# Newton's iteration for both head groups of a batch in one chain, with landmark and U transposes as whole tiles

## The chip, the cores and the metric

The kernel runs on one core of a Trainium2 chip. The metric is the device time of one execution in microseconds (us); lower is better. Before the change it is 927.63 us, the median of three runs (926.26 to 928.45).

## What is computed

Three stages follow each other; all arrays are float32.

```
Nystrom attention, batch 4, heads 8, seq 576, head_dim 64, m = 32:
  q_lm, k_lm = mean of q, k over 18 neighbouring rows        (32 landmarks a head)
  A = softmax(q k_lm^T)   B = softmax(q_lm k_lm^T)   C = softmax(q_lm k^T)
  Z = B^T / (norm1(B) * norminf(B) + 1e-6);  6 times: Z = 2 Z - Z B Z
  x = A Z C v                       -> 2304 tokens x 512
two gated layers, d_model 512, d_ff 1536:
  x = (silu(x wg1) * (x wv1)) wo1;  out = (sigmoid(x wg2) * (x wv2)) wo2
```

The factor U = Z C v (32 x 64 a head) is multiplied into the first layer's weights, so that the first layer reads A straight: x wg1 = A (U wg1).

## The kernel before

A batch has two head groups g of four heads, and 32 rows of each head fill a quarter of the 128 partitions. The work on one (b, g) is the generator `attention`, cut in two parts. The front part, called F in the order of work, does this: sums of 18 rows on VectorE (`lm`, L107); the landmark sums transposed on TensorE by two ordinary matmuls with the identity (`lt`, L111), so that the result stands on both partition halves; nine 128x128 transposes of k and nine of q (`tp`, L121); scores of C (`cs`), of B (`bm`) and of A (`as`); the exponentials; transposes of C's exponentials (`et`, L207); and C v (`cv`, L213). The back part, B, normalises B and finds the two norms with small VectorE instructions (L220 to L237), runs Newton's iteration (`nw`, L240 to L261), transposes U (`ut`, L265) into `UT[b]`, and finishes A (`a_steps`, L144 to L158) between the iterations.

Newton's iteration is carried on [Z^T-like 32 columns | U 64 columns] together, 96 columns a head. One product is four matmuls of 32x32 weights, one for each head, each on its own 32 rows and 32 columns of the array; one VectorE instruction of 96 columns reads the result and makes the next operand. There are seven products and seven such instructions to a chain, and each needs the one before.

After B of both groups, `uw_steps` (L391, word U, tile `pu`) multiplies UT[b] by the chunk of the first layer's weights: eight matmuls of 64x32 weights and 512 columns. The weights of two heads lie on the two partition halves, and `half` (L386) says which half a head has; for heads 4 to 7 `load_in` (L307) loads the halves swapped. Then G (`gv1_steps`, tiles `pg`, `pv`) and O (`o1_steps`, tile `po`) are the first layer, in matmuls of 128x128 weights and 288 columns, three for each product (high and low parts). The second layer has the same form.

The order in which the work is recorded is written out by hand as words (L570): letter, then (b, g) for F and B, or (chunk, batch) for U, G and O; words joined by + take turns.

```
first = (
    "I0+F00 F01 B00+F10 B01 U00 F11 J0 B10 G00 I1 F20 U10 J1 O00 G10 B11 O10 U01 G01 F21 U11 "
    "B20+F30+B21 O01 G11 B30+F31 U02 O11 G02 B31 U12 O02 G12 U03 O12 G03 U13 O03 G13"
)
```

A scheduler then orders the recorded instructions on each engine by its own costs; that order is fixed when the program runs. I and J wait for the conversion of weights, which fills in (`wfill`) between steps. Attention tiles in PSUM use the tags gv (3 banks), n (1), o (2) and a (2). All loads are issued on SP.

Of the kernel before, what the change touches and what calls it, by code (L numbers as in the profile page):

```python
# [5 lines left out]
F32 = mybir.dt.float32  # L6
# [8 lines left out]
def nystrom_moe_kernel(tc, q, k, v, wg1, wv1, wo1, wg2, wv2, wo2, out):  # L15
    nc = tc.nc
# [39 lines left out]
    UT = [cst.tile([P, H, M], F32, tag=f"ut{b}", name=f"ut{b}") for b in range(B)]  # L56
# [33 lines left out]
    def attention(b, g):  # L90
# [3 lines left out]
        def small(tag, shape, bufs=2):  # L94
            return att.tile(shape, F32, tag=tag, name=f"{tag}{nm_}", bufs=bufs)

        def pst(shape, nm):

            tag = "n" if nm in ("nw", "ut") else "a"
            if b == 0:  # L100
                tag = {"tp": "gv", "cs": "o", "as": "o", "nw": "no"[g], "ut": "no"[g]}.get(nm, tag)
            return ptile(shape, tag, f"{nm}_{nm_}")

        def lm_steps(which):
            src = inq[which, b, g]
            lm = small("lm", [P, D])
            nc.vector.tensor_reduce(lm, src.rearrange("p u d -> p d u"), axis=AX.X, op=ALU.add)  # L107
            yield
            ps = pst([P, P], "lt")
            for w in range(2):  # L110
                mm(ps[D * w:D * w + D], lm, ident)  # L111
            bdt = small("bd" + which, [P, 2, P], 1)
# [14 lines left out]
        def a_scores(bdk, qT, s):  # L127

            amx = small("amx", [P, L])
            for i0, i1 in ((0, 5), (5, NU)):  # L130
                ps = pst([P, 5, 2 * M], "as")
                for i in range(i0, i1):
                    for h in range(4):
                        hs = slice(M * h, M * h + M)
                        mm(ps[hs, i - i0].rearrange("p (w m) -> p w m", w=2), qT[:, i, hs], bdk[:, :, hs])
                x = flat(ps[:, 0:i1 - i0]).rearrange("p (u m) -> p u m", m=M)
                us = slice(2 * i0, 2 * i1)
                nc.vector.tensor_reduce(amx[:, us], x, axis=AX.X, op=ALU.max)
                nc.vector.tensor_tensor(s[:, us], x, amx[:, us, None].to_broadcast([P, 2 * (i1 - i0), M]),
                                        op=ALU.subtract)  # L140
                nc.scalar.activation(s[:, us], s[:, us], AF.Exp)
                yield

        def a_steps(s):  # L144
            asm = small("asm", [P, L])
            nc.vector.tensor_reduce(asm, s, axis=AX.X, op=ALU.add)
            nc.vector.tensor_scalar(asm, asm, 1e-9, None, op0=ALU.add)
            nc.vector.reciprocal(asm, asm)
            yield
            nc.vector.tensor_tensor(s, s, asm[:, :, None].to_broadcast([P, L, M]), op=ALU.mult)  # L150
            yield
            at = small("at", [P, S], 1)
            nc.vector.transpose(out=at, in_=flat(s))
            hi, lo = AH[:, 8 * g + b], AH[:, 8 * g + 4 + b]
            nc.scalar.copy(hi, at)
            nc.vector.tensor_tensor(lo, at, hi.bitcast(F32), op=ALU.subtract)
            AT[b, g, 0] = hi
            AT[b, g, 1] = lo  # L158
            yield
# [4 lines left out]
        cmx = small("cmx", [P, 2])
        csm = small("csm", [P, 2])
        nmx = small("nmx", [P, 1])
        e = small("e", [P, 3, 2, M, 3], 1)
# [16 lines left out]
        bs = small("bs", [P, M])  # L184
        bmx = small("bmx", [P, 1])
        bsm = small("bsm", [P, 1])
        ps = pst([P, M], "bm")
# [22 lines left out]
        ps = pst([P, D], "cv")  # L210
# [4 lines left out]
        nc.vector.tensor_scalar(BC[:, M:M + D], ps, rc, None, op0=ALU.mult)  # L215
        load_next(b, g, "v")
        yield
        yield "back"
# [3 lines left out]
        nc.vector.tensor_scalar(BC[:, 0:M], bs, bsm, None, op0=ALU.mult)  # L222
        bmt = small("bmt", [P, M])
        nc.vector.transpose(out=bmt, in_=BC[:, 0:M])
        nrm = small("nrm", [P, 2])
        nc.vector.tensor_reduce(nrm[:, 0:1], BC[:, 0:M], axis=AX.X, op=ALU.add)
        nc.vector.tensor_reduce(nrm[:, 1:2], bmt, axis=AX.X, op=ALU.add)
        yield
        nb = small("nb", [P, 2, M])
        nc.vector.tensor_copy(nb, nrm[:, :, None].to_broadcast([P, 2, M]))  # L230
        nbt = small("nbt", [P, 2, M])
        nc.vector.transpose(out=flat(nbt), in_=flat(nb))
        nmax = small("nmax", [P, 2])
        nc.vector.tensor_reduce(nmax, nbt, axis=AX.X, op=ALU.max)
        rr = small("rr", [P, 1])
        nc.vector.tensor_scalar(rr, nmax[:, 0:1], nmax[:, 1:2], 1e-6, op0=ALU.mult, op1=ALU.add)
        nc.vector.reciprocal(rr, rr)  # L237


        def prod(x):  # L240
            ps = pst([P, 96], "nw")
            for h in range(4):
                hs = slice(M * h, M * h + M)
                mm(ps[hs], x[hs, 0:M], x[hs])
            return ps

        ga = a_steps(sx)
        ps = prod(BC)
        RW = small("rw", [P, 96], 4)
        nc.vector.tensor_scalar(RW, ps, rr, None, op0=ALU.mult)  # L250
# [12 lines left out]
        ps = pst([P, P], "ut")
# [4 lines left out]
        yield from ga  # L268
# [385 lines left out]
```

## Time and profile before

| what | value |
|---|---|
| median of the runs | 927.63 us |
| the profiled execution's own time | 925.59 us |
| span of its instructions on the core | 923.8 us |
| TensorE busy | 896.7 us (97%) |
| VectorE busy | 549.0 us (59%) |
| ScalarE busy | 389.3 us (42%) |
| mean granted TensorE clock | 0.987 of full |

PE is TensorE's matmuls, PEld its weight loads, DVE is VectorE, ACT ScalarE, POOL GpSimd, SP SyncE, which issues the loads. Busy time of PE is a modelled one, since matmuls overlap: where rows follow each other without a gap, the time from one start to the next is what a group takes. A float32 matmul gives two records in the trace, a float32 transpose and a matmul of the float32r type one. The granted clock is a share of 2.4 GHz; at 0.50 the array runs at 1.2 GHz.

### The profile page before, as it was taken

The page shows a single profiled execution, that of the slowest core. Times are in us where ns is not written, and L with a number is a line of the kernel's source. Part 1 is how long each engine was busy: PE and PEld are TensorE (multiplying, and loading weights), DVE is VectorE, ACT ScalarE, POOL GpSimd, SP SyncE. Part 2 cuts the span into 40 slices and gives each one's busy share as a digit, 9 for nine tenths or more (in the row PEclk, how much of TensorE's full clock was granted, in tenths as well). Part 3 has the DMA queues.
Part 4 walks back from the last instruction along what each step waited for, and adds up shares of the span by engine and source line. Part 5 has one row for each costly group of instructions (what it writes and reads, how often), then busy time and mean ns, then how long its engine had stood idle before and what let it go on. Part 6 is the DMA issues. An engine that isn't in the chain of part 4 may idle for free.

```text
span 923.8 us, 16229 instructions
## 1 busy us (share of the span) xinstructions
PE 896.7 (97%) x6664; PEld 747.5 (81%) x6664; DVE 549.0 (59%) x1165; ACT 389.3 (42%) x833; POOL 0.7 (0%) x6
## 2 busy tenths in 40 slices
PE   6789999999999999999999999999999999999997
PEld 4456866677989989899898888888888888888886
DVE  7799958647677668858972135347237336323243
ACT  6569655545645336536753343125116114111111
POOL 0000000000000000000000000000000000000000
PEclk9689999999999999999999999999999999999999
DMA  8664211003322104302101013004004000000132
GB/s 275 194 195 159 83 53 47 8 1 92 120 64 89 48 2 128 102 1 92 47 3 44 1 46 92 0 1 137 1 1 137 1 0 23 1 1 1 46 92 69
DMA packets 26698, 57.67 MB, mean 62 GB/s; under 512 B 3840, under 2 KB 6912, under 8 KB 26624
## 3 DMA queue, kind: packets, MB, share of 16 engines
q1 hardware_dynamic: 24896, 54.28, 18.9%
q10 hardware_dynamic: 1728, 2.36, 1.1%
q8 instruction: 52, 0.85, 0.4%
q14 instruction: 22, 0.18, 0.1%
HBM read 51.90 MB, written 4.72 MB: 61 GB/s over the span
## 4 chain that ended last, share of the span: by engine, by line
PE 91%; DVE 5%; ACT 2%; DMA 1%; issue 1%; SPq 0%; DVEq 0%; ACTq 0%
PE po L62 33%; PE pg L62 24%; PE pv L62 24%; PE pu L62 3%; PE nw L62 2%; PE tp L121 2%; DVE lm L107 1%; PE cs L62 1%; DMA kin<-in_k_dram 1%; PE cv L62 1%; PE as L62 1%; PE et L207 1%; PE lt L62 0%; DVE hl L327 0%; DVE cv L295 0%
## 5 line engine op out<-in xcount | busy, mean ns | idle before, releaser
L62 PE MATMUL po<-hh,wo 128*128 128x288 f32 x768 | 162.8, 303 | 1.0 <-DVE uw L327 0.7
L492 DVE TENSOR_TENSOR hf<-hf,pv 128x512 f32<-128x512 f32 (+1 forms) x60 | 38.0, 634 | 194.1 <-PE pv L62 191.5
L62 PE MATMUL po<-wo,h 128*128 128x512 f32 x648 | 152.2, 390 | 0.0
L62 PEld LDWEIGHTS po<-wo,h 128*128 128x128 f32 x648 | 121.2, 188 | 25.3 <-ACT h L326 0.3
L62 PEld LDWEIGHTS po<-hh,wo 128*128 128x128 f32 x768 | 123.2, 188 | 20.5 <-issue 13.7
L62 PE MATMUL pg<-AH,w 128*128 128x512 f32 (+1 forms) x480 | 136.2, 368 | 0.0
L62 PE MATMUL pv<-AH,w 128*128 128x512 f32 (+1 forms) x480 | 136.1, 368 | 0.0
L62 PE MATMUL po<-hl,wo 128*128 128x288 f32 x384 | 115.1, 300 | 0.3 <-DVE hl L327 0.3
L491 ACT ACTIVATE hf<-pg 128x512 f32<-128x512 f32 (+1 forms) x60 | 33.1, 552 | 165.2 <-PE pg L62 157.0
L62 PE MATMUL pg<-AH,uw 128*128 128x288 f32 x576 | 98.9, 298 | 2.5 <-ACT uw L326 2.4
L62 PEld LDWEIGHTS pg<-AH,w 128*128 128x128 f32 x480 | 87.4, 189 | 15.4
L62 PEld LDWEIGHTS pv<-AH,w 128*128 128x128 f32 x480 | 87.1, 189 | 14.9
L62 PE MATMUL pv<-AH,uw 128*128 128x288 f32 x576 | 95.9, 296 | 0.0
L62 PEld LDWEIGHTS pg<-AH,uw 128*128 128x128 f32 x576 | 83.2, 188 | 9.2 <-ACT uw L326 5.3
L326 ACT CAST h<-hf 128x512 fp32r<-128x512 f32 (+1 forms) x60 | 34.6, 576 | 123.6 <-DVE hf L492 123.6
L513 DVE TENSOR_TENSOR oacc<-po,oacc 128x512 f32<-128x512 f32 x90 | 61.9, 691 | 41.1 <-PE po L62 39.9
L62 PEld LDWEIGHTS pv<-AH,uw 128*128 128x128 f32 x576 | 82.7, 188 | 2.9 <-ACT bdk L114 0.8
L62 PE MATMUL pg<-x1l,w 128*128 128x512 f32 x192 | 74.8, 389 | 0.0
L62 PE MATMUL pv<-x1l,w 128*128 128x512 f32 x192 | 74.8, 389 | 0.0
L62 PEld LDWEIGHTS po<-hl,wo 128*128 128x128 f32 x384 | 72.3, 188 | 2.7 <-issue 1.1
L447 DVE TENSOR_TENSOR acc<-po,acc 128x288 f32<-128x288 f32 x128 | 55.8, 453 | 16.8 <-PE po L62 16.0
L419 ACT ACTIVATE sg<-pg 128x288 f32<-128x288 f32 x96 | 39.1, 407 | 51.8 <-PE pg L62 51.2
(106 smaller groups left out, 1093.9 us busy)
## 6 DMA issues: line engine op xcount, KB each, us to landing
raw<-in_moe_w_out_dram SPq DMA_DIRECT2D x24, 512.0 KB, 4.3
raw<-in_moe_w_gate_dram SPq DMA_DIRECT2D x36, 256.0 KB, 3.2
raw<-in_moe_w_val_dram SPq DMA_DIRECT2D x36, 256.0 KB, 3.5
kin<-in_k_dram SPq DMA_DIRECT2D x8, 576.0 KB, 4.7
qin<-in_q_dram SPq DMA_DIRECT2D x8, 576.0 KB, 5.5
vin<-in_v_dram SPq DMA_DIRECT2D x8, 576.0 KB, 4.6
raw<-in_moe_w_gate_dram SPq DMA_DIRECT2D x24, 128.0 KB, 2.9
raw<-in_moe_w_val_dram SPq DMA_DIRECT2D x24, 128.0 KB, 3.0
```

Source lines behind the costliest of these rows:

```text
L62: nc.tensor.matmul(o, l, r, start=start, stop=stop, skip_group_check=True)
L107: nc.vector.tensor_reduce(lm, src.rearrange("p u d -> p d u"), axis=AX.X, op=ALU.add)
L121: nc.tensor.transpose(ps[:, j], flat(src[:, 2 * u:2 * u + 2]), ident)
L207: nc.tensor.transpose(ps[:, j, :], flat(e[:, r // 2, r % 2]), ident)
L326: nc.scalar.copy(hi, x)
L419: nc.scalar.activation(sg, pss[0], AF.Silu)
L447: nc.vector.tensor_tensor(sl, ps, sl, op=ALU.add)
L491: nc.scalar.activation(h, pss[0], AF.Sigmoid)
L492: nc.vector.tensor_tensor(h, h, pss[1], op=ALU.mult)
L513: nc.vector.tensor_tensor(acc, ps, acc, op=ALU.add)
```

## The change

One back part now serves both head groups of a batch. Its tiles have the group as another dimension: B's rows `bs` (128x2x32), `BC` (128x2x96), the iterate `RW` (128x2x96), `rr` (128x2). One product is eight matmuls: four for group 0 and four for group 1, on the same four places of the array. One VectorE instruction of 192 columns follows. The words B00, B01 and so on become B0 to B3, and stand after both fronts. In the front part A's scores move behind C v. The sum of landmarks is written twice side by side by a ScalarE copy, so that one 128x128 transpose gives both halves. U of both groups is one 128x128 tile and one transpose; so group 0 lies on partitions 0 to 63 and group 1 on 64 to 127, and the first layer's weights are loaded that way, by four transfers of 64 rows each for every tile pair. UT[b] has half the columns that it had.

```
-            lm = small("lm", [P, D])
-            nc.vector.tensor_reduce(lm, src.rearrange("p u d -> p d u"), axis=AX.X, op=ALU.add)
+            lm = sm("lm", [P, 2, D])
+            nc.vector.tensor_reduce(lm[:, 0], src.rearrange("p u d -> p d u"), axis=AX.X, op=ALU.add)
+            nc.scalar.copy(lm[:, 1], lm[:, 0])
-            for w in range(2):
-                mm(ps[D * w:D * w + D], lm, ident)
+            nc.tensor.transpose(ps, flat(lm), ident)
...
         def prod(x):
-            ps = pst([P, 96], "nw")
-            for h in range(4):
-                hs = slice(M * h, M * h + M)
-                mm(ps[hs], x[hs, 0:M], x[hs])
+            ps = pst(b, [P, 2, 96], "nw")
+            for g in range(2):
+                for h in range(4):
+                    hs = slice(M * h, M * h + M)
+                    mm(ps[hs, g], x[hs, g, 0:M], x[hs, g])
             return ps
-        RW = small("rw", [P, 96], 4)
-        nc.vector.tensor_scalar(RW, ps, rr, None, op0=ALU.mult)
+        RW = sm("rw", [P, 2, 96], 3)
+        nc.vector.tensor_tensor(RW, ps, rr[:, :, None].to_broadcast([P, 2, 96]), op=ALU.mult)
...
-        for w in range(2):
-            mm(ps[D * w:D * w + D], UU, ident)
-        nc.vector.tensor_copy(flat(UT[b][:, 4 * g:4 * g + 4]), ps)
+        nc.tensor.transpose(ps, flat(UU), ident)
+        nc.vector.tensor_copy(flat(UT[b]), ps)
...
-            if layer == 0 and kk >= 2:
-                nc.sync.dma_start(t[0:D, j], x[D:P])
-                nc.sync.dma_start(t[D:P, j], x[0:D])
+            if layer == 0:
+                for g in range(2):
+                    r0 = D * (4 * g + kk)
+                    nc.sync.dma_start(t[D * g:D * g + D, j], w[r0:r0 + D, 2 * FC * c:2 * FC * (c + 1)])
...
-        for h in range(H):
-            rows = slice(D * half(h), D * half(h) + D)
-            mm(pss[h // 4][M * (h % 4):M * (h % 4) + M, :], UT[b][rows, h, :],
-               W1[c][rows, h // 2].rearrange("p a b -> p (a b)"))
+        for g in range(2):
+            rows = slice(D * g, D * g + D)
+            for h in range(4):
+                mm(pss[g][M * h:M * h + M, :], UT[b][rows, h, :], W1[c][rows, h].rearrange("p a b -> p (a b)"))
...
-        "I0+F00 F01 B00+F10 B01 U00 F11 J0 B10 G00 I1 F20 U10 J1 O00 G10 B11 O10 U01 G01 F21 U11 "
-        "B20+F30+B21 O01 G11 B30+F31 U02 O11 G02 B31 U12 O02 G12 U03 O12 G03 U13 O03 G13"
+        "I0+F00 F01 B0+F10 U00 F11 J0 B1 G00 I1 F20 U10 J1 O00 G10 O10 U01 G01 F21 U11 "
+        "B2+F30 O01 G11 F31 U02 O11 G02 B3 U12 O02 G12 U03 O12 G03 U13 O03 G13"
```

How the order of instructions moves is shown at two places. The numbers in the rows' names: the first after the tile's name is the head group (for `pu`, `pg`, `po` the batch, then the group or token half); an x at the end counts instructions of one row.

TensorE before, at the end of batch 0's second chain, up to U of chunk 0 and batch 0 (`pu`):

```order
L62 MATMUL cv_0_714<-vin_0_490,eT_0_703 32x64 x24
L62 MATMUL nw_1_796<-rw_1_790 32x96 x4
L62 MATMUL lt_1_843<-ident,lm_1_841 64x128 x2
L121 MATMUL tp_1_850<-ident,kin_1_345 128x128 x2
L62 MATMUL nw_1_803<-rw_1_801 32x96 x4
L121 MATMUL tp_1_850<-ident,kin_1_345 128x128
L121 MATMUL tp_1_855<-ident,kin_1_345 128x128 x3
L62 MATMUL nw_1_810<-rw_1_808 32x96 x4
L121 MATMUL tp_1_860<-ident,kin_1_345 128x128 x3
L62 MATMUL lt_1_869<-ident,lm_1_867 64x128 x2
L62 MATMUL ut_1_817<-ident,uu_1_815 64x128 x2
L62 MATMUL pu_0_0_821<-w_0_97,ut_82 32x512 x4
```

TensorE after the change, at the same place:

```order
L62 MATMUL nw_0_634<-rw_625 32x96 x8
L62 MATMUL bm_0_687<-bdk_0_519,bdq_0_613 32x32 x4
L185 MATMUL et_0_699<-ident,e_0_670 96x128 x2
L287 MATMUL ut_0_650<-ident,rw_643 128x128
L185 MATMUL et_0_699<-ident,e_0_670 96x128
L185 MATMUL et_0_704<-ident,e_0_670 96x128 x3
L62 MATMUL cv_0_709<-vin_0_447,eT_0_698 32x64 x12
L62 MATMUL pu_0_0_783<-w_0_97,ut_82 32x512
L62 MATMUL cv_0_709<-vin_0_447,eT_0_698 32x64 x12
L62 MATMUL as_0_739<-bdk_0_519,kq_0_628 32x64 x20
L62 MATMUL as_0_763<-bdk_0_519,kq_0_628 32x64 x16
L62 MATMUL pu_0_0_783<-w_0_97,ut_82 32x512 x3
```

Before, the landmarks and key transposes of F11 (`lt_1`, `tp_1`) stood ahead of `pu`, and F10 was done; now none of F11 stands ahead of it, and half of C v and all of A's scores of F10 stand behind its first matmul.

TensorE before, in batch 2, where the chains of both groups (`nw_0`, `nw_1`) and the front of batch 3's group 0 take turns:

```order
L62 MATMUL nw_1_2107<-rw_1_2088 32x96 x4
L121 MATMUL tp_0_2235<-ident,qin_0_1287 128x128 x3
L62 MATMUL po_0_1_2395<-hh_0_1_1821,wo_0_98 128x288
L62 MATMUL po_0_1_2395<-hl_0_1_1822,wo_0_98 128x288
L62 MATMUL po_0_1_2395<-hh_0_1_1843,wo_0_98 128x288 x2
L62 MATMUL cs_0_2244<-kq_0_2101,bdq_0_2192 32x288
L62 MATMUL nw_0_2118<-rw_0_2095 32x96 x4
L62 MATMUL cs_0_2244<-kq_0_2101,bdq_0_2192 32x288 x3
L62 MATMUL cs_0_2250<-kq_0_2101,bdq_0_2192 32x288
L62 MATMUL nw_1_2131<-rw_1_2112 32x96 x4
L62 MATMUL cs_0_2250<-kq_0_2101,bdq_0_2192 32x288 x3
```

TensorE after the change, in the same batch (here `nw_0` is both groups):

```order
L62 MATMUL nw_0_2054<-rw_2045 32x96 x8
L135 MATMUL tp_0_2111<-ident,qin_0_1288 128x128
L62 MATMUL cs_0_2127<-kq_0_1993,bdq_0_2071 32x288 x4
L62 MATMUL po_0_1_2283<-hh_0_1_1745,wo_0_98 128x288 x2
L62 MATMUL po_0_1_2283<-hl_0_1_1746,wo_0_98 128x288
L62 MATMUL po_0_1_2283<-hh_0_1_1767,wo_0_98 128x288 x2
L62 MATMUL nw_0_2074<-rw_2063 32x96 x8
L62 MATMUL po_0_1_2283<-hl_0_1_1768,wo_0_98 128x288
L62 MATMUL po_0_1_2291<-hh_0_1_1745,wo_0_98 128x288
L62 MATMUL cs_0_2133<-kq_0_1993,bdq_0_2071 32x288 x4
L62 MATMUL po_0_1_2291<-hh_0_1_1745,wo_0_98 128x288
L62 MATMUL nw_0_2092<-rw_2083 32x96 x8
```

Groups of four `nw` matmuls became groups of eight, half as many; the scores `cs` that were cut into one and three matmuls stand whole.

## Rows read from the trace of the kernel before

**Rows 1.** The page: TensorE's busy time, and the chain that ended last by engine.

```profile
PE 896.7 (97%) x6664; PEld 747.5 (81%) x6664; DVE 549.0 (59%) x1165; ACT 389.3 (42%) x833; POOL 0.7 (0%) x6
PE 91%; DVE 5%; ACT 2%; DMA 1%; issue 1%; SPq 0%; DVEq 0%; ACTq 0%
```

**Rows 2.** Windows: stretch and its length, busy us of each engine, granted clock, DMA.

```profile
core 0: us, PE busy (x) PEld busy (x) DVE busy (x) ACT busy (x) POOL busy (x), PEclk, DMA share, GB/s
0.00:60.10 60.10, 42.50 (x665) 27.60 (x665) 47.03 (x114) 34.00 (x84) 0.70 (x6) 0.80 0.71 223
36.00:44.00 8.00, 8.00 (x70) 4.19 (x60) 3.81 (x16) 3.16 (x8) 0.00 (x0) 0.50 0.51 147
60.10:85.60 25.50, 24.59 (x322) 14.28 (x320) 23.89 (x62) 23.17 (x47) 0.00 (x0) 1.00 0.49 157
85.60:226.50 140.90, 138.85 (x1649) 106.09 (x1649) 101.18 (x272) 80.91 (x188) 0.00 (x0) 1.00 0.20 58
```

**Rows 3.** Timeline of TensorE: start, duration, line, tiles, count; batch 0's first U.

```profile
60.14 1.52 PE L62 MATMUL pu<-w,ut 64*32 64x512 f32 x16
```

**Rows 4.** Timeline of TensorE: one Newton product between matmuls of O.

```profile
105.57 0.29 PE L62 MATMUL po<-hh,wo 128*128 128x288 f32 x1
105.85 0.37 PE L62 MATMUL nw<-rw 32*32 32x96 f32 x8
106.15 0.40 PE L62 MATMUL po<-hh,wo 128*128 128x288 f32 x1
106.39 0.29 PE L62 MATMUL po<-hl,wo 128*128 128x288 f32 x1
106.52 0.42 PE L62 MATMUL po<-hh,wo 128*128 128x288 f32 x2
```

**Rows 5.** Timeline of TensorE: scores of C, one half of them, and both.

```profile
127.73 0.69 PE L62 MATMUL cs<-kq,bdq 128*32 128x288 f32 x8
...
87.49 1.18 PE L62 MATMUL cs<-kq,bdq 128*32 128x288 f32 x16
```

**Rows 6.** Timeline of TensorE: a landmark transposition; one, three and six transposes.

```profile
107.01 0.44 PE L62 MATMUL lt<-ident,lm 128*64 128x128 f32 x4
107.38 0.44 PE L121 MATMUL tp<-ident,kin 128*128 128x128 f32 x2
...
116.06 0.27 PE L121 MATMUL tp<-ident,kin 128*128 128x128 f32 x1
...
160.81 0.55 PE L121 MATMUL tp<-ident,kin 128*128 128x128 f32 x3
...
166.71 0.87 PE L121 MATMUL tp<-ident,kin 128*128 128x128 f32 x6
```

**Rows 7.** Timeline of TensorE: a cut piece of C's scores; A's scores and C v whole.

```profile
145.54 0.67 PE L62 MATMUL cs<-kq,bdq 128*32 128x288 f32 x2
...
178.98 1.26 PE L62 MATMUL as<-bdk,kq 128*32 128x64 f32 x72
...
98.83 0.88 PE L62 MATMUL cv<-vin,eT 96*32 96x64 f32 x48
```

**Rows 8.** Groups of VectorE: Newton's step, and a reduction for the norms; count, busy, mean ns.

```profile
L255 DVE SCALAR_TENSOR_TENSOR rw<-rw,nw 128x96 f32<-128x96 f32 x40 | 10.0, 251 | 9.4 <-PE nw L62 8.9
L226 DVE TENSOR_REDUCE nrm<-bc 128x1 f32<-128x32 f32 x8 | 1.2, 147 | 0.0
```

**Rows 9.** Timeline of TensorE: two Newton products of one chain that follow each other.

```profile
57.88 0.37 PE L62 MATMUL nw<-rw 32*32 32x96 f32 x8
...
58.78 0.37 PE L62 MATMUL nw<-rw 32*32 32x96 f32 x8
```

**Rows 10.** Timeline of TensorE: U, one matmul of it alone, and all eight.

```profile
126.28 1.04 PE L62 MATMUL pu<-w,ut 64*32 64x512 f32 x2
...
116.90 1.09 PE L62 MATMUL pu<-w,ut 64*32 64x512 f32 x16
```

**Rows 11.** Waits of SP's own queue: line, waited for, us in total, times, longest.

```profile
SPq L322 <- ACT cv L293: 379.9, 14, 63.4
```

More of the change, by code (lines that the diff above doesn't have):

```diff
@@ L54, in nystrom_moe_kernel @@
         nc.vector.memset(pmask[64 * h:64 * h + 64, h:h + 1], QSC)
-    UT = [cst.tile([P, H, M], F32, tag=f"ut{b}", name=f"ut{b}") for b in range(B)]
+    UT = [cst.tile([P, 4, M], F32, tag=f"ut{b}", name=f"ut{b}") for b in range(B)]
     AT = {}
@@ L125, in lm_steps @@
             return bdt, t
[L127 to L132, printed above, removed]
-                    for h in range(4):
-                        hs = slice(M * h, M * h + M)
[L135 to L159, printed above, removed]
         bdk, kT = yield from lm_steps("k")
         bdq, qT = yield from lm_steps("q")
[L164 to L167, printed above, removed]
+        if g == 0:
+            BS[b] = (small("bs", [P, 2, M], b), small("bsm", [P, 2], b), small("bc", [P, 2, 96], b))
+        bs, bsm, BC = BS[b]
+        cmx = sm("cmx", [P, 2])
+        csm = sm("csm", [P, 2])
+        nmx = sm("nmx", [P, 1])
+        e = sm("e", [P, 3, 2, M, 3], 1)
         pcs = []
         for w in range(2):
-            ps = pst([P, NU, M], "cs")
+            ps = pst(b, [P, NU, M], "cs", g)
             for h in range(4):
@@ L182, in attention @@
         yield
[L184 to L187, printed above, removed]
+        bmx = sm("bmx", [P, 1])
+        ps = pst(b, [P, M], "bm", g)
         for h in range(4):
@@ new lines, in a_steps @@
+    def a_steps(b, g):
+        s = SX[b, g]
+        asm = small("asm", [P, L], f"{b}_{g}")
+        nc.vector.tensor_reduce(asm, s, axis=AX.X, op=ALU.add)
+        nc.vector.tensor_scalar(asm, asm, 1e-9, None, op0=ALU.add)
+        nc.vector.reciprocal(asm, asm)
+        yield
+        nc.vector.tensor_tensor(s, s, asm[:, :, None].to_broadcast([P, L, M]), op=ALU.mult)
+        yield
+        at = flat(small("sx", [P, L, M], f"{b}_{g}t", 3))
+        nc.vector.transpose(out=at, in_=flat(s))
+        hi, lo = AH[:, 8 * g + b], AH[:, 8 * g + 4 + b]
+        nc.scalar.copy(hi, at)
+        nc.vector.tensor_tensor(lo, at, hi.bitcast(F32), op=ALU.subtract)
+        AT[b, g, 0] = hi
+        AT[b, g, 1] = lo
+        yield
@@ L220, in attention, with back, sm @@
+    def back(b):
+        def sm(tag, shape, bufs=2):
+            return small(tag, shape, b, bufs)
+        bs, bsm, BC = BS[b]
         nc.vector.tensor_scalar(bsm, bsm, 1e-9, None, op0=ALU.add)
         nc.vector.reciprocal(bsm, bsm)
[L222 to L226, printed above, removed]
@@ L227, in attention @@
-        nc.vector.tensor_reduce(nrm[:, 1:2], bmt, axis=AX.X, op=ALU.add)
+        nc.vector.tensor_tensor(bs, bs, bsm[:, :, None].to_broadcast([P, 2, M]), op=ALU.mult)
+        nc.scalar.copy(BC[:, :, 0:M], bs)
+        bmt = sm("bmt", [P, 2, M])
+        nc.vector.transpose(out=flat(bmt), in_=flat(bs))
+        nrm = sm("nrm", [P, 2, 2])
+        nc.vector.tensor_reduce(nrm[:, 0], bs, axis=AX.X, op=ALU.add)
+        nc.vector.tensor_reduce(nrm[:, 1], bmt, axis=AX.X, op=ALU.add)
         yield
-        nb = small("nb", [P, 2, M])
@@ L524, in nystrom_moe_kernel @@
     wfill = []
-    def step(fill, n=1):
-        while n and fill:
-            try:
-                next(fill[0])
-                n -= 1
-            except StopIteration:
-                fill.pop(0)
     def main(gen):
@@ L536, in main @@
             step(wfill, 2)
-    atts = {x: attention(*x) for x in AORDER}
-    def front(b, g):
-        for x in atts[b, g]:
-            if x == "back":
-                return
-            yield
     def weights_to(c, part):
```

108 lines of the change are left out of this document (65 added, 43 removed).

## The prediction

> **What bounds the kernel now.** I read the page first. TensorE is busy 97% of the span and makes up 91% of the chain that ended last [rows 1], so time is won where TensorE's own stream gets shorter or where it stands less. Busy time alone doesn't say which, so the windows come next [rows 2]. They show three stages. In the first 60.1 us TensorE is busy 42.5 us and runs at a mean clock of 0.80; VectorE is busy 47.0 us. This is the start, in which batch 0's attention has to end before the first U. From 60.1 to 85.6 us TensorE, VectorE (23.9 of 25.5) and ScalarE (23.2) are all near full. From 85.6 to 226.5 us TensorE is busy 138.9 of 140.9 us. So behind 60.1 us TensorE stands for only 3.0 us (0.9 and 2.1): there every piece of its stream counts in full. The change touches nothing behind the last U of batch 3 that differs on TensorE, so the rest of the span keeps its length. The reader is to see that the same edit has to be priced by two measures: ahead of U00 (at 60.14 us [rows 3]) by the chain to U, behind it by TensorE's starts.
>
> **The change part by part.** Negative is time won.
>
> (a) Newton's products behind U00. Ahead of U00 stand both chains of batch 0; behind it 6 chains of 7 products, 42 groups; now 21. A group takes 0.30 us from its start to the next (105.85 to 106.15) [rows 4]. The four matmuls of the second head group use the same four places of the array, so they queue: the second set of four score matmuls adds 0.49 us (1.18 less 0.69) for 288 columns [rows 5], so 96 columns add 0.16, and a new group is 0.46. A pair saves 0.14. Besides, each group that cuts a run of 128x128 matmuls slows its neighbours: they take 0.28 and 0.24 where one in the run takes 0.13 [rows 4], 0.26 for a cut. About half of the groups stand in such a run, so a pair saves 0.27 and 21 pairs 5.7 us. Bounds: 2.9 (no cut saved) and 8.4 (every one).
>
> (b) Landmarks. Ten of the 16 come behind U00. One takes 0.37 us (107.01 to 107.38); three more transposes in a run add 0.32, so 0.11 each, which is what a transposition beside the others costs [rows 6]. 10 x 0.26 is 2.6. Bounds: 1.0, if each stands alone (0.27), and 5.2, if each also spares a cut.
>
> (c) U's transposition has the same shape. Six times 0.37 go and three times 0.11 come, 1.9, and three cuts of the O run go, of which I count 0.3: 2.2. Bounds 1.4 and 3.0.
>
> (d) Cuts of other groups. Where two chains alternated, scores were cut: a lone score matmul takes 0.67 us [rows 7], while four together take 0.69 [rows 5]. In batch 2 the two cuts end (the order above); as three pieces instead of two halves they cost 0.8. Bounds: nothing (the new groups are cut by transposes in two places) and 1.4.
>
> Sum on TensorE behind U00: -11.3, bounds -5.3 and -18.0.
>
> (e) The start. The chain to U goes through VectorE. Of two back parts ahead of U00 one goes: seven steps of 0.25 us and 13 small instructions between 0.15 and 0.25 [rows 8], about 4.1. The remaining seven are 96 columns wider; from 32 columns (147 ns) to 96 (251 ns) a column costs 1.6 ns, so 0.15 each, 1.1. I take -3.0, with VectorE's idle time as it was. Bounds: nothing, since VectorE idles 13.1 of 60.1 us anyway, and a whole chain of seven iterations at 0.90 us (57.88 to 58.78) [rows 9], -6.3. Nearest is the first way of counting, since from 36 to 44 us it is TensorE that is full, at half clock [rows 2].
>
> (f) Work that moves behind U00. Ahead of it stood two landmarks (0.74) and nine key transposes (1.1) of F11, and C v (0.81) and A's scores (1.19) of F10 [rows 6, 7]. All of it now stands behind the first U matmul: +3.9. This has one answer, and it eats the start's gain.
>
> (g) Added waits. G10 waits for weights and for U's split on VectorE and ScalarE, both full from 60.1 to 85.6 [rows 2], and ScalarE gets a copy for every landmark and two copies of U's operands. VectorE has one back part less there. I count +0.5; bounds 0 and 4. Queued behind such a wait on TensorE is all of G10.
>
> (h) Nothing: the first layer's loads are 24 issues more on SP, but SP's queue stands 380 us for converted buffers [rows 11]; the cover is the three raw tiles, and without it the first chunk would come some 1 to 2 us later, still ahead of U00. The eight U matmuls now go by partition halves; they use the same eight places, and eight take 1.09 us where one takes 1.04 [rows 10]. If they went one half after the other it would be 0.97 a U.
>
> Sum: -11.3 - 3.0 + 3.9 + 0.5 = -9.9 us, with ends at -20.4 and +2.6. The profiled execution took 925.6 us, so 915.7; the median of the runs stands 2.0 above it, so 917.7.
>
> **A rule against it.** From 36 to 44 us TensorE is busy without a break, with transposes and Newton products, and the granted clock stays at 0.50, which is 1.2 GHz [rows 2]. The change makes 16 landmarks and 4 U's transposes too, and thins the start's stream. The Trainium skill, "TensorE: Matmul & The Clock Gate", section "Part 4: PE-mode transpose", says that transposes do not count as busy work for the clock as matmuls do; the trace agrees. By it the half clock would last longer, which is the first rival.
>
> **Rivals.**
>
> 1. The half clock reaches past U00. Between the transposed U and the first `pg` now stand C v 0.81, a U matmul 0.97, scores 1.19, the other seven 1.0 and four transposes 0.5, some 4.5 us [rows 6, 7, 10]; at half clock they take 4.5 more: 922.2. For it: the 8 us at 0.50, and fewer chains to fill the start. Against: the clock was at full from 60.1 on [rows 2], after scores and C v, which come as late now. Chance 0.20.
>
> 2. Slower: one chain alone leaves TensorE standing. An iteration took 0.90 us [rows 9]; with the second set (0.16) and the wider step (0.15) it is 1.21, and TensorE itself works 0.46 of that. Where fewer than 0.75 us of other work stand between two groups, TensorE waits in order, and all behind it. If nothing stood between in the 21 behind U00, they would cost 15.8: 933.5. It turns slower than before from 13 such iterations on. For it: two chains no longer fill each other. Against: in batch 2 the new order has 1.0 us and more between groups (scores of 0.6 and O matmuls of 0.13). Chance 0.10.
>
> 3. A better start: the second chain falls off the path to U as a whole, -6.3 in (e): 914.4. For it: TensorE was the full engine at half clock. Against: lm sums and weights still fill VectorE. Chance 0.17.
>
> 4. U's matmuls go half after half: 24 x 0.97 is 23, so 941. Four column places with the same rows overlapped in the scores [rows 5], which speaks against it; 0.02. That the change does something else than it says is out, by the order shown; 0.01 for the unforeseen.
>
> **How the numbers follow.** The forecast 917.7 has 0.50, with a range of its own of 913 to 922. The asked range takes in rivals 1 and 3 and the bounds of (a) and (g) partly: 912 to 925; rivals 2 and 4 and the far ends are left out. About 0.2% (1.9 us) is what a measurement of this kernel can tell from no change. Faster by more: the forecast, rivals 1 and 3, less their slow tails: 0.84. Within it 0.05: slow tails of rival 1 and of (g). Slower 0.11: rivals 2 and 4, unless mild.
>
> **What would show it.** In the new profile, groups of 16 `nw` records should take 0.46 us from start to next start, the landmark one record and 0.11 us in a run; U00 should start at 56 to 58 us; from U00 to the last U of batch 3 TensorE should stand 3 to 5 us in all. It is wrong if `nw` waits for VectorE in most iterations (rival 2), if the clock is still 0.50 at `pu` (rival 1), if U takes 2 us (rival 4), or if the first `pg` of G10 comes later than 85 us.

## The result and the profile after

The changed kernel takes 918.66 us, the median of four runs (917.74 to 920.14), beside 928.0 us for the kernel before on the same chip: a ratio of 0.9904 with the interval [0.9884, 0.9924], 9.3 us faster. A second comparison gave 0.9910 [0.9892, 0.9927]. The forecast was 917.7 us (912 to 925), so time and sign were right. Of the steps behind them some were right to within some tenths and others were not; the time came out in part because errors cancelled.

The page of the profiled execution (917.74 us, span 915.9 us), busy time and share:

```profile
PE 877.8 (96%) x6588; PEld 741.9 (81%) x6588; DVE 542.2 (59%) x1093; ACT 391.7 (43%) x853; POOL 0.7 (0%) x6
```

TensorE has 18.9 us less to do than before, of which 11 lie ahead of U00 (42.5 to 31.2). Part of that moved behind U00, and part is half clock: ahead of U00 TensorE worked 21.8 us at 0.50 before and 11.9 us after. The windows of the profile after, cut at the first U matmul, at the first `pg`, at 85 us and at U of chunk 1 and batch 3 (columns as in [rows 2]):

```profile
0.00:56.30 56.30, 31.24 (x528) 21.46 (x528) 44.36 (x90) 32.30 (x87) 0.70 (x6) 0.79 0.73 221
56.30:60.79 4.49, 4.00 (x119) 1.88 (x114) 3.15 (x8) 2.51 (x6) 0.00 (x0) 1.00 0.50 135
60.79:85.00 24.21, 22.29 (x292) 16.12 (x292) 22.09 (x52) 23.95 (x55) 0.00 (x0) 1.00 0.64 190
85.00:218.50 133.50, 129.45 (x1627) 103.00 (x1618) 95.74 (x226) 81.37 (x193) 0.00 (x0) 1.00 0.20 58
```

Set against [rows 2, 3]: U00 starts at 56.30 instead of 60.14 us (-3.84); from there to the last U of batch 3 it is 162.2 instead of 166.3 us (-4.13); behind that 697.4 in both. The two add up to the span's difference, 7.9 us, to within a tenth. (The profiled execution before lay 2.4 us under the median of 928.0, the one after 0.9 under its own; so the medians differ by 9.3.) In the middle stretch TensorE's own work falls by 7.6 us, 163.4 to 155.7, but it stands 6.5 us instead of 3.0.

TensorE in the profile after, at the places the prediction speaks of: the way from U00 to the first `pg`, a product between transposes, and a landmark in a run:

```profile
56.30 1.04 PE L62 MATMUL pu<-w,ut 64*32 64x512 f32 x2
57.27 0.54 PE L62 MATMUL cv<-vin,eT 96*32 96x64 f32 x24
57.63 1.48 PE L62 MATMUL as<-bdk,kq 128*32 128x64 f32 x72
59.04 1.08 PE L62 MATMUL pu<-w,ut 64*32 64x512 f32 x14
...
60.79 0.40 PE L62 MATMUL pg<-AH,uw 128*128 128x288 f32 x1 [0.41 <-ACT uw L350]
...
84.64 0.53 PE L62 MATMUL nw<-rw 32*32 32x96 f32 x16
85.10 0.55 PE L135 MATMUL tp<-ident,kin 128*128 128x128 f32 x3
...
102.02 0.27 PE L125 MATMUL lt<-ident,lm 128*128 128x128 f32 x1
102.13 0.49 PE L135 MATMUL tp<-ident,kin 128*128 128x128 f32 x3
```

A product of both head groups takes 0.46 us from start to start (84.64 to 85.10), a landmark 0.11 (102.02 to 102.13): these two are the prediction's prices. From U00 to the first `pg` it is 4.49 us, the prediction's 4.5, but made up otherwise: only half of C v stands there (24 records), and 0.5 us of it is waiting. What TensorE waits for behind U00 is new. The waits of TensorE after the change, from U00 to U of chunk 1 and batch 3 (total us, times, longest):

```profile
PE cv L62 <- ACT eT L186: 1.6, 1, 1.6
PE as L62 <- DVE bc L193: 1.2, 3, 0.8
PE pv L62 <- ACT sg L439: 1.2, 1, 1.2
PE pg L62 <- ACT uw L350: 1.1, 2, 0.7
PE tp L135 <- ACT bdk L128: 0.6, 1, 0.6
PE pg L62 <- DVE h L441: 0.4, 1, 0.4
```

Before, the same view has three lines: `pg` for `uw` 1.7, `tp` for `bdk` 0.5 and `pu` for `w` 0.3. The first three lines here are most of the loss. They lie at 77.67 us (`cv`), mostly at 99.20 (`as`) and at 103.78 (`pv`); of the 3.5 us that TensorE stands longer, 1.5 lie ahead of about 85 us and 2.0 behind (4.05 instead of 2.05 us). The two longest, with what ScalarE did ahead of them:

```profile
77.67 0.92 PE L62 MATMUL cv<-vin,eT 96*32 96x64 f32 x48 [1.55 <-ACT eT L186]
...
103.78 1.06 PE L62 MATMUL pv<-AH,uw 128*128 128x288 f32 x6 [1.16 <-ACT sg L439]
```

```profile
73.91 1.28 ACT L439 ACT_TABLE_LOAD   x1
75.64 1.28 ACT L174 ACT_TABLE_LOAD   x1
77.16 0.83 ACT L186 COPY eT<-et 96x384 f32<-96x384 f32 x2
...
102.02 1.28 ACT L439 ACT_TABLE_LOAD   x1
103.31 0.41 ACT L439 ACTIVATE sg<-pg 128x288 f32<-128x288 f32 x1
```

An `ACT_TABLE_LOAD` is an instruction of ScalarE, 1.28 us long. It stands in this kernel where ScalarE turns from exponentials (L162, L174, L210) to the gate's function (L439) or back. Both long waits are for work that ScalarE began 0.01 and 0.24 us behind such a load. The kernel before has as many of them (15 in the span), but none in the 1.5 us ahead of any of its waits above 0.3 us.

By kind of matmul, from U00 to the last U of batch 3 (each record counted from its start to the next start, less idle time; worked out from all records of both traces):

| us on TensorE | before | after | change | forecast, step |
|---|---|---|---|---|
| `nw` | 12.84 | 10.26 | -2.6 | -2.9: (a), the groups themselves |
| `pg`, `pv`, `po` | 95.14 | 93.77 | -1.4 | -2.7: (a), the cuts |
| `lt` | 2.96 (8 landmarks) | 1.24 (10) | -1.7 | -1.9: (b), -2.6, and (f), +0.7 |
| `ut` | 2.21 | 0.08 | -2.1 | -2.2: (c) |
| `cs` | 6.74 | 5.95 | -0.8 | -0.8: (d) |
| `as`, `cv`, `tp` | 22.51 | 23.63 | +1.1 | +3.1: (f) |
| `et`, `bm`, `pu` | 20.95 | 20.80 | -0.1 | |
| sum | 163.36 | 155.73 | -7.6 | -7.4 |

### The profile page after: what moved, and what is told of

It is laid out like the page before. It is cut to its first block, busy times and chain, and to the rows that moved or that the text cites. A ratio compares the mean times of both kernels' runs of the same rounds, so it can differ in the third digit from the quotient of the medians.

```text
span 915.9 us, 16047 instructions
## 1 busy us (share of the span) xinstructions
PE 877.8 (96%) x6588; PEld 741.9 (81%) x6588; DVE 542.2 (59%) x1093; ACT 391.7 (43%) x853; POOL 0.7 (0%) x6
## 4 chain that ended last, share of the span: by engine, by line
PE 88%; DVE 5%; ACT 4%; DMA 1%; issue 1%; SPq 0%; ACTq 0%
PE po L62 33%; PE pg L62 24%; PE pv L62 23%; PE pu L62 3%; PE tp L135 2%; PE nw L62 1%; DMA qin<-in_q_dram 1%; DVE lm L121 1%; PE cs L62 1%; ACT e L162 1%; PE as L62 1%; DVE hl L351 0%; ACT L162 0%; PE et L185 0%; DVE h L441 0%
## 5 line engine op out<-in xcount | busy, mean ns | idle before, releaser
L62 PEld LDWEIGHTS po<-hh,wo 128*128 128x128 f32 x768 | 123.0, 188 | 21.1 <-issue 14.4
L511 ACT ACTIVATE hf<-pg 128x512 f32<-128x512 f32 (+1 forms) x60 | 33.2, 554 | 165.4 <-PE pg L62 158.3
L439 ACT ACTIVATE sg<-pg 128x288 f32<-128x288 f32 x96 | 39.2, 409 | 51.7 <-PE pg L62 51.1
```

Of the source, the lines that this page charges most:

```text
L62: nc.tensor.matmul(o, l, r, start=start, stop=stop, skip_group_check=True)
L439: nc.scalar.activation(sg, pss[0], AF.Silu)
L511: nc.scalar.activation(h, pss[0], AF.Sigmoid)
```

## The experiments

All are edits of the changed kernel unless the name says otherwise. The ratio is to the kernel before, with its 95% interval; the other columns are of the profiled execution: start of U00, TensorE's own work from U00 to the last U of batch 3, how long it stands there, and how much of that stretch lies at a granted clock of 0.50. In brackets stands an estimate of what the half clock added to the work: the start-to-start times of the records in it, less the mean of the same kinds of matmul in the rest of that kernel's stretch.

| kernel | median us | ratio | U00 | work | stands | at 0.50 |
|---|---|---|---|---|---|---|
| before | 928.0 | 1 | 60.1 | 163.4 | 3.0 | 0 |
| changed | 918.66 | 0.9904 [0.9884, 0.9924] | 56.3 | 155.7 | 6.5 | 0 |
| changed, again | 918.43 | 0.9910 [0.9892, 0.9927] | 55.9 | 155.7 | 6.5 | 0 |
| before_tiles | 920.53 | 0.9930 [0.9916, 0.9945] | 57.7 | 161.0 | 3.0 | 0 |
| tiles_undone | 923.96 | 0.9974 [0.9964, 0.9984] | 57.0 | 159.8 | 7.2 | 3.4 (1.1) |
| two_chains | 930.98 | 1.0041 [1.0026, 1.0056] | 61.2 | 161.5 | 8.9 | 6.8 (3.0) |
| scores_first | 920.11 | 0.9934 [0.9919, 0.9948] | 55.9 | 157.3 | 6.3 | 3.4 (1.3) |
| pool_copy | 921.71 | 0.9937 [0.9920, 0.9955] | 58.4 | 158.3 | 6.7 | 6.8 (2.4) |
| v_ahead | 923.46 | 0.9961 [0.9946, 0.9977] | 53.0 | 165.4 | 6.1 | 14.4 (7.3) |
| v_fill | 921.08 | 0.9933 [0.9920, 0.9947] | 56.7 | 157.0 | 8.8 | 6.8 (3.0) |
| v_fill2 | 921.50 | 0.9940 [0.9926, 0.9954] | 56.3 | 156.1 | 9.2 | 3.4 (1.5) |
| one_load | 1039.79 | 1.1222 [1.1204, 1.1241] | 95.6 | | | |
| fill_after | 922.66 | 0.9952 [0.9936, 0.9968] | 71.4 | 147.1 | 4.7 | 0 |
| fill_before | 935.04 | 1.0086 [1.0069, 1.0103] | 80.1 | 153.5 | 3.1 | 0 |

None beats the changed kernel; the intervals of before_tiles, scores_first, pool_copy, v_fill and v_fill2 overlap with one or both of its own. The work column holds what the order puts behind U00, so where U00 moves against the rest of the batch, work moves with it. The last column matters for all that follows: behind U00 the clock stayed at 1.00 in the changed kernel and in its repeat, but fell in seven of its variants, so part of their loss is the clock and not the edit's own work.

**Newton's chain split again.**

```
-        ps = prod(BC)
-        nc.vector.tensor_tensor(RW, ps, rr[:, :, None].to_broadcast([P, 2, 96]), op=ALU.mult)
+        def chain(g):
+            ps = prod(BC[:, g], g)
+            nc.vector.tensor_scalar(RW, ps, rr[:, g:g + 1], None, op0=ALU.mult)
...
+        for it in range(7):
+            for ch in chains:
+                next(ch)
```

> The changed kernel with its products and VectorE steps split by head group again (two chains that take turns; norms, landmarks, U's transposition, W1 and the order of words stay joint). My theory, that a product costs TensorE its start-to-start time and the cuts in its neighbours: 21 more groups behind U00, each 0.30 x 2 against 0.46 and 0.13 for a cut, +5.5 us behind U00, and seven more VectorE steps ahead of it, up to +1: 918.7 + 5.5 to 6.5, 924 to 925. If the gain came from fewer cuts only partly (what the trace after shows, 2.6 us in the groups and about 1.4 in their neighbours), +4: 922.7. Rival, that the order of work made the gain and not the products: within 1 us of 918.7, since two chains also fill each other's waits.

The ratio stands 1.3% above the changed kernel's, about 12 us: twice what was expected. The windows of this kernel, cut at its U00 and its last U of batch 3:

```profile
0.00:61.15 61.15, 35.83 (x624) 23.44 (x624) 47.51 (x103) 34.15 (x89) 0.70 (x6) 0.78 0.71 212
61.15:231.54 170.39, 161.50 (x1926) 121.86 (x1925) 122.64 (x300) 123.79 (x263) 0.00 (x0) 0.98 0.25 73
```

TensorE's work behind U00 is 161.5 against 155.7 us: +5.8. That this is step (a)'s price (5.7) is a coincidence, for two parts of the stretch ran at half clock:

```profile
82.20:85.40 3.20, 3.03 (x47) 2.56 (x47) 3.20 (x10) 2.69 (x6) 0.00 (x0) 0.50 0.72 189
140.20:143.50 3.30, 3.30 (x82) 2.35 (x74) 2.94 (x7) 1.11 (x4) 0.00 (x0) 0.50 0.55 147
```

By the estimate above the clock makes 3.0 of the 5.8, and some 2.8 are left for the groups and their cuts, half of what was priced. `nw` has 2.6 of the 5.8, `po` 3.8, `cs` 2.0, and `pu` gives 2.5 back. The rest of the 13 us of span is the start, +4.85, and waits, +2.4. The rival's number, within 1 us, is out, but the run isn't the products alone: its order gives ScalarE 29 table loads instead of 15. How the start's 4.85 come about the run doesn't say, since 3.15 us more of VectorE's work lie in it and its seven added steps are only about 1.

**Landmarks and U in two matmuls again.**

```
-            nc.scalar.copy(lm[:, 1], lm[:, 0])
-            nc.tensor.transpose(ps, flat(lm), ident)
+            for w in range(2):
+                mm(ps[D * w:D * w + D], lm, ident)
...
-        nc.tensor.transpose(ps, flat(UU), ident)
+        for g in range(2):
+            mm(ps[D * g:D * g + D], UU[:, g], ident)
```

> The changed kernel with the landmarks transposed by two ordinary matmuls of 64 columns again (no second copy on ScalarE), and U by two such matmuls. My theory: ten landmarks and three U's behind U00 at 0.37 instead of 0.11 to 0.12: +3.3 us, 922.0. Rival: the 16 ScalarE copies of 0.24 us cost waits, since ScalarE ends three of the stalls behind U00 (1.55, 1.16 and 0.41 us in the trace after); without them up to 2 us of these go, and the sum is +1.3, 920.

```profile
0.00:57.01 57.01, 32.90 (x525) 22.21 (x525) 44.27 (x90) 30.79 (x75) 0.70 (x6) 0.79 0.73 220
57.01:223.99 166.98, 159.75 (x2086) 124.15 (x2085) 121.14 (x284) 108.73 (x247) 0.00 (x0) 0.99 0.27 78
```

The kernel loses 0.6 to 0.7%, about 6 us: +4.0 us of TensorE's work (expected +3.3), 0.7 in the start, and 0.8 more waiting, although ScalarE had 16 copies less. `lt` and `ut` have 3.5 of the work; some 1.1 of it is half clock from 79.8 to 83.2 us. The rival, by which ScalarE's copies make the waits, gets nothing from this: C v's wait behind the pair of table loads is 2.4 us here instead of 1.55.

**The landmarks alone, in the kernel before** (`nc.scalar.copy` and one transposition, as in the change).

> The kernel before with nothing changed but the landmarks: the sum copied by ScalarE and one 128x128 transposition. My theory: the eight landmarks behind U00 go from 0.37 to 0.12 us, -2.0 us (bounds -1 and -4 with the cuts), 926.0 against 928.0. Rival: ScalarE's copies and the order give it back: within 0.5 us of 928.0.

```profile
0.00:57.67 57.67, 36.70 (x641) 24.83 (x641) 47.37 (x114) 34.65 (x92) 0.70 (x6) 0.85 0.76 234
57.67:221.66 163.99, 160.97 (x1937) 119.75 (x1935) 124.74 (x333) 110.53 (x246) 0.00 (x0) 1.00 0.25 74
```

This was the surprise: 0.70%, 6.5 us of the change's 9, three times the expectation. The profiled executions are 5.0 us apart. Behind U00 the span gains 2.3 of them (`lt` -1.9), as reckoned. Another 2.5 us lie in the start, with VectorE's work as before (47.4 us): the prediction gave the landmarks nothing there. TensorE is busy 36.7 instead of 42.5 us ahead of U00, at a mean clock of 0.85 instead of 0.80. The landmarks themselves can't be all of that: two of those ahead of U00 took 0.70 us each at half clock before, and one takes 0.47 now. How the rest divides between the order and the clock is open. Together with tiles_undone (the joint chain without the new landmarks and U, -0.26%) it makes -0.96%, close to the whole change. But the parts don't add up in general: undone alone, the joint products cost 1.3% (two_chains).

**The loads of the first layer, two by one.**

```
-                for g in range(2):
-                    r0 = D * (4 * g + kk)
-                    nc.sync.dma_start(t[D * g:D * g + D, j], w[r0:r0 + D, 2 * FC * c:2 * FC * (c + 1)])
+                x = w[:, 2 * FC * c:2 * FC * (c + 1)].rearrange("(g r) f -> g r f", g=2)
+                nc.sync.dma_start(t[:, j], x[:, D * kk:D * kk + D])
```

> The changed kernel with each 128-row piece of the first layer's gate or value weights loaded by one transfer of both halves instead of two of 64 rows; same bytes, same places, 48 issues less on SP. The prediction's step (h), that the loads cost nothing: within 1 us of 918.7. Rival: the issues hold v for F01, which SP issued at 29.6 us instead of 25.1 and for which C v waits 3.5 us in the trace after; then v is issued by 26 us, C v starts 3 us earlier and U00 by up to 3 us earlier than 56.3: 915.7.

Neither: 12% slower. The first row is this kernel's from 30 to 38 us, the second the changed kernel's from 13 to 16, when in both only such weights are on their way (the last two columns are the share of the DMA engines and GB/s):

```profile
30.00:38.00 8.00, 0.00 (x0) 0.00 (x0) 1.69 (x3) 1.42 (x4) 0.00 (x0) 0.50 0.13 50
```

```profile
13.00:16.00 3.00, 1.65 (x15) 1.29 (x13) 2.68 (x6) 1.42 (x5) 0.00 (x0) 1.00 1.01 264
```

A share of 0.13 is two of 16 DMA engines (0.125), and 50 GB/s is a fifth of 264. The source's outermost dimension became the two head groups. The Trainium skill, "DMA: Bandwidth & Descriptors", section "Why a DMA increments its semaphore by 16 and not by 1", says that a transfer is spread over the largest number of engines, up to 16, that divides the slowest dimension of both sides; by it two engines move these, and the row agrees. So the run tells nothing of the number of issues. No run does; the next one asks after their order.

**v ahead of the weights.**

```
-        load_next(b, g, "v")
+        with tc.high_priority(offset=60):
+            load_next(b, g, "v")
```

> The changed kernel with the loads of v recorded at a higher priority, so that v for F01 stands ahead of the last four weight transfers on SP instead of behind them; nothing else. The prediction's step (h), that the loads' order costs nothing, since VectorE sets the start: within 0.7 us of 918.7, U00 within 0.7 us of 56.3. Rival: C v of F01 waits 3.5 us for v at 35.5 us in the trace after, and its result on VectorE comes at 42.5 only; with v issued at 25 instead of 29.6 us U00 comes by 2 to 3.5 us earlier: 915 to 917.

In the changed kernel F01's C v waits for v, and what VectorE makes of it comes late. SP, TensorE and VectorE of the changed kernel:

```profile
29.63 0.53 SPq L71 DMA_DIRECT2D vin<-in_v_dram  x1
```

```profile
35.52 1.51 PE L62 MATMUL cv<-vin,eT 96*32 96x64 f32 x48 [3.46 <-DMA vin<-in_v_dram]
...
42.84 0.55 PE L62 MATMUL nw<-bc 32*32 32x96 f32 x8 [5.40 <-DVE bc L193]
```

```profile
42.52 0.27 DVE L193 TENSOR_SCALAR bc<-cv,rc 128x64 f32<-128x64 f32 x1
```

In v_ahead SP issues v at 25.34, but C v still starts at 35.03: v lands hardly sooner, beside the other loads, and that part of the rival was wrong. What moved is VectorE's order, in which `bc` now stands at 37.86 instead of 42.52, and U00 comes at 53.01, 3.3 us earlier, as the rival said. And yet the kernel is 5 us slower. TensorE of v_ahead around U00, and its windows:

```profile
50.69 0.86 PE L62 MATMUL nw<-rw 32*32 32x96 f32 x16 [2.35 <-DVE rw L279]
...
53.01 1.91 PE L62 MATMUL pu<-w,ut 64*32 64x512 f32 x2
...
62.56 0.40 PE L62 MATMUL pg<-AH,uw 128*128 128x288 f32 x1 [0.39 <-ACT uw L351]
```

```profile
48.00:50.00 2.00, 0.34 (x16) 0.12 (x8) 2.00 (x2) 0.00 (x0) 0.00 (x0) 1.00 1.01 274
50.00:61.00 11.00, 10.23 (x162) 5.43 (x167) 5.09 (x16) 4.26 (x12) 0.00 (x0) 0.53 0.10 26
81.20:87.80 6.60, 5.88 (x99) 4.27 (x91) 6.36 (x18) 5.40 (x14) 0.00 (x0) 0.50 0.71 172
```

TensorE stands 2.35 us for VectorE, the clock falls to 0.50, and U00, C v and A's scores run at 1.2 GHz. From U00 to the first `pg` it is 9.55 us instead of 4.49: the prediction's first rival, in a kernel other than the one it was written for. Not all of the 5.1 us is the clock, since three more transposes and the other half of C v stand in it. With the earlier U00 the first `pg` is only 1.8 us late. The rest is lost behind it, where TensorE's work is 156.2 instead of 151.7 us and the clock falls a second time (the last row).

**The same with TensorE kept busy.** Ten matmuls of the identity with itself fill that gap (v_fill); eight more fill the wait for v (v_fill2). Their result is not used.

```
+            if b == 0 and it == 4:
+                idle(10)
```

> The kernel of the run v_ahead with ten identity matmuls more (128x128, result unused) behind the sixth product of batch 0's chain, where TensorE stood 2.35 us and after which the clock was 0.50 to 0.59 from 50 to 60 us. If that half clock is what v_ahead lost (its first pg came 9.5 us behind U00 instead of 4.5): clock 1.00 from 50 to 60, U00 at 53 to 54, first pg by 58.5, 919 or lower. If the clock is not the cause, or the ten hold up the chain: first pg at 62 or later and 923 or more.

> As v_fill, and eight more such matmuls ahead of F01's C v, where TensorE stands 3.6 us for v, so that the clock rises before 36 us. If clock and chain add up: U00 one to three us earlier than in v_fill, 916 to 918. Rival: VectorE, which is busy 4.00 of 4 us from 28 to 36, sets these products, and eight matmuls at half clock only stand in the way: no gain over v_fill.

```profile
48.00:50.00 2.00, 2.00 (x41) 1.25 (x30) 1.73 (x4) 0.00 (x0) 0.00 (x0) 1.00 0.96 327
50.00:61.00 11.00, 9.56 (x202) 7.00 (x201) 10.02 (x24) 7.53 (x21) 0.00 (x0) 1.00 0.49 121
```

In v_fill the clock stays at 1.00 here. U00 itself comes no sooner (56.7 us), but more of the work that followed it now stands ahead of it, and the first `pg` starts at 58.54, 4.0 us ahead of v_ahead and 2.25 ahead of the changed kernel. That settles what v_ahead lost up to this point. But the kernel is only 2.4 us faster than v_ahead, and slower than the changed one. It stands 8.8 us behind U00, with five stalls of 0.5 to 1.3 us between 74 and 84 us, and then the clock falls here too:

```profile
82.40:89.10 6.70, 5.82 (x46) 2.94 (x47) 3.76 (x10) 3.84 (x10) 0.00 (x0) 0.50 0.49 160
```

From the first `pg` on TensorE works 155.4 us instead of 151.7, and by the estimate above 3.0 of these 3.7 us are this half clock. A start won by 2 us is lost again to waits and to the clock behind them. The eight more of v_fill2 brought nothing.

**The clock held up throughout**, by 100 such matmuls ahead of U00, in the changed kernel and in the one before.

> The changed kernel with 100 matmuls of the identity with itself (128x128, result unused) put on TensorE where the order leaves it idle ahead of U00. They cost 100 x 0.16 us at full clock in stretches where TensorE stood 25 us. If they hold the clock up from 24 to 48 us, where it stood at 0.50 to 0.54 after the change, TensorE's 11.7 us of work there get shorter by up to 5.9; VectorE is busy throughout 32 to 44, so I expect U00 1 to 3 us earlier than 56.3: 916 to 918. If VectorE alone sets the start: U00 within 0.7 of 56.3 or later.

> The same 100 matmuls in the kernel before, where the clock stood at 0.50 in most of 34 to 57 us. If the start's gain of 3.8 us was the clock and not VectorE's shorter chains (the clock after the change was full from 48 us on, before it was half until 57), U00 comes 3 to 5 us earlier than 60.1: 923 to 925. If it was VectorE: U00 within 1 us of 60.1, 927 to 928.

The clock was 1.00 from 24 to 62 us in both, but U00 came at 71.4 and 80.1 us. I had mispriced the filling: ten take 2.50 us in v_fill, so 100 take 25 and not 16, and they stood in the way. These two runs leave open whether the start's 3.8 us are the clock's. For the clock: just ahead of U00 the kernel before ran at 0.50 (first row), the changed kernel at 1.00. Against it: the repeat of the changed kernel had less half clock in its start than the first (mean 0.85 instead of 0.79, second row), and U00 came only 0.4 us earlier.

```profile
50.20:56.80 6.60, 5.59 (x117) 3.81 (x105) 6.43 (x9) 2.17 (x7) 0.00 (x0) 0.50 0.46 113
```

```profile
0.00:55.92 55.92, 30.72 (x527) 21.45 (x527) 44.28 (x90) 32.36 (x87) 0.70 (x6) 0.85 0.78 224
```

**ScalarE's copies on GpSimd** (`nc.gpsimd.tensor_copy` for the landmarks' second copy).

> The changed kernel with the landmarks' second copies on GpSimd instead of ScalarE. Theory that ScalarE's added copies make the new stalls behind U00 (ScalarE is busy 24.6 of 25 us from 60 to 85, and ends stalls of 1.55, 1.16 and 0.41): four copies of 0.24 us go from that stretch, -1 to -2 us: 917 or so. Rival, that the stalls come from the order and from what ScalarE had to do before too: within 0.7 us of 918.7; and if GpSimd's copy takes over 1 us, later U: slower by 1.

No gain: 921.71 us, with runs from 918.9 to 922.8, of which the profiled one is the longest. ScalarE was busy 21.6 instead of 23.95 us from 60.8 to 85, but TensorE stands as long as in the changed kernel (6.7 us), U00 comes 2.1 us later, and the clock was 0.50 from 79.8 to 86.7 us. With these copies gone from ScalarE, C v still waits 2.1 us behind the pair of table loads. So the added copies are not what makes the stalls.

**A's scores ahead of C v again.**

> The changed kernel with A's scores recorded ahead of the transposed exponentials and C v in the front part, as in the kernel before. Theory that the stalls behind U00 belong to this part of the change: where C v waits 1.55 us for eT at 77.7 us, A's scores are no longer left to run behind it, but have to wait less too; with the scores ahead TensorE waits at A's scores for the exponentials instead, as before the change, and the four stalls of front parts (1.55, 0.18, 0.82, 0.24 us) go by half: -1.5; U00 comes 1.2 us later, since F10's scores move ahead of it, and as much less stands behind it, so the sum is 916 to 918. Rival: the stalls come from ScalarE and VectorE being full from 60 to 85 us; they only change their place: within 1 us of 918.5.

The waits of the first list above go (`cv` for `eT` from 1.6 to 0.9, `as` for `bc` to nothing), and others come: `et` waits 1.6 us for VectorE's `sx`, `bm` 0.7 for `e`. The sum is 6.3 us instead of 6.5. They change their place, as the rival said; U00 did not come later. The median is 1.6 us above 918.5, not within 1; the work is 1.6 us longer, and half clock from 81.0 to 84.5 us makes some 1.3 of that.

**The changed kernel again.**

> The changed kernel itself, beside the others on one chip: a ratio of 0.990 to the kernel before, as the first comparison gave (0.9904).

U00 at 55.9, work 155.7, stands 6.5: the figures above repeat within 0.4 us.

## Why the prediction was right, and where it was not

- **(a) to (d), TensorE's work behind U00: right as a sum.** With the moved work of (f) it was -7.4 us, measured -7.6. (b), (c) and (d) hold within 0.2 us ((b) with the two moved landmarks). In (a) the groups gave 2.6 of 2.9. The cuts gave 1.4 of 2.7 in `pg`, `pv` and `po`; more of them may lie in the matmuls of the next step. Undone in two_chains, the joint products are worth some 2.8 us once the half clock is taken off, where 5.7 were priced.
- **(f): right in sum with the cuts, not by itself.** `as`, `cv` and `tp` took 1.1 us more, where 3.1 were reckoned. (f) puts all of C v behind the first U matmul, but half of it (0.4 us) stayed ahead. The other 1.6 us may be cuts that these kinds were spared (a record of C v fell from 0.020 to 0.016 us); then the cuts gave 3.0 of 2.7. The trace doesn't separate the two. So the sum may have come out in part by luck. The way from U00 to the first `pg` came out (4.49 against 4.5) with half of C v missing and 0.5 us of waiting in its place.
- **(e), the start: right in size (-3.0 against -3.8), incomplete in its reason.** VectorE's busy time ahead of U00 fell by 2.7 us (47.0 to 44.4) and its idle time from 13.1 to 11.9, where (e) took it as unchanged. But before_tiles got 2.5 us with VectorE's work unchanged, from landmarks that (b) counted only behind U00. A term for them is missing. How they, VectorE's shorter chain, the order and the clock share the 3.8 us is open: in ten kernels (all but one_load and the two with 100 matmuls), U00 came between 53.0 and 61.2 us, 10.3 to 14.0 us above VectorE's busy time.
- **(g), added waits: the step that failed.** It took +0.5 us (0 to 4), at G10. TensorE stands 3.5 us longer, and at other places: at F fronts' C v and scores and at `pv`. G10 itself was on time: its first `pg`, by the count of `pg` records, came at 80.4 us, in the kernel before at 85.6. Its bound was taken from ScalarE and VectorE being full up to 85.6 us, its value was not. They are full there after the change too (23.95 and 22.1 of 24.21 us), but that doesn't explain all of it: 2.0 of the 3.5 us lie behind 85 us, where ScalarE is busy 61% and VectorE 72%. Neither ScalarE's copies (tiles_undone, pool_copy) nor the order of the front part (scores_first) is what the sum hangs on. The trace points at ScalarE's table loads of 1.28 us: the two longest waits, 1.55 and 1.16 us, stand right behind them, and C v's wait behind the same pair was 2.1 to 2.4 us in tiles_undone, two_chains, pool_copy and v_ahead. Their number didn't grow; where the order puts them did change. No run moved or removed one, so this is read from the trace and not shown.
- **(h), loads at nothing: not borne out for the order.** The place of v among the loads moved VectorE's order and U00 by 3.3 us. The 380 us of SP's waits [rows 11], on which (h) rests, lie wholly behind the first 60 us. In v_ahead half clock took more than that gain back, so the forecast lost nothing by the step, but for another reason than it gave.
- **Rival 1, half clock past U00**: not in this kernel, where it was full from 48 us on. TensorE ran from 42.84 to 48.8 us without a break, on transposes and Newton's products alone, and the clock rose from 0.50 to 1.00 at 48.2 us, within that stretch. So the rule cited from the Trainium skill, "TensorE: Matmul & The Clock Gate", section "Part 4: PE-mode transpose", did not decide here, with products between the transposes; no run has transposes alone.
- **Rival 2, one chain that TensorE waits for**: 0.01 us of waiting before `nw` behind U00. **Rival 4**: 14 records of U in 1.08 us, so the halves overlap.
- What was to show it: 0.46, 0.11 and U00 at 56.3 came; "TensorE stands 3 to 5 us" did not (6.5).

The time was right in part by luck. For the profiled execution the gain was 7.9 us where 9.9 were forecast (917.7 instead of 915.7): a start better by 0.8 and 0.2 more of work saved paid for a third of the 3.0 us of waits that (g) missed. The median came within 1.0 us of the forecast because it stood only 0.9 us above the profiled execution, where the prediction had added 2.0.

## What to carry to other kernels

Where an engine is full, price an edit by its start-to-start time and its cuts, from rows of the same stretch: the start-to-start prices came out within some tenths, the cuts only in sum with the work that moved. Price the same edit in every stage where it stands: the landmarks' edit alone gained as much ahead of U00 as behind it, and the prediction had counted it behind only. When the bound engine gets less to do, part of the gain can turn into waits; here it was 3.5 of 11.5 us. Look for them engine by engine, at single long instructions such as ScalarE's table loads, and not at busy shares alone. And before reading an experiment's loss as its edit's price, read the granted clock behind it: in seven variants here it fell where the changed kernel's did not, and made up to about 3 us of the loss behind the first `pg`.

## What the runs showed of the hardware that was not expected

- A load whose source has an outermost dimension of two used 0.13 of the DMA engines and moved 50 GB/s; the changed kernel, with loads of 64 rows, moved 264 GB/s at a share of 1.01 while it loaded such weights.
- In v_ahead TensorE stood 2.35 us ahead of U00, and the clock was 0.50 from 50.3 to 60.6 us; ten unused matmuls of 0.25 us each in the gap kept it at 1.00 there, and the first `pg` came 4.0 us earlier (v_fill).
- The clock fell to 0.50 well inside the full stretch too, for 3.4 to 6.8 us from about 80 to 82 us on (in two_chains again from 140 us), in seven variants; in the changed kernel and its repeat it did not.
- A table load took 1.28 us of ScalarE, each time.
- A 128x64 copy took 0.34 us on GpSimd and 0.24 on ScalarE.
